# Zeros' products, alpha's operations and the first factors in the opening of a fused attention and snake-activation kernel

## Chip, cores and metric

One core of a Trainium2 chip runs the whole program. The metric is the time of one execution on the device in microseconds (us); a kernel is run three times or more, and the median counts. One more execution is taken by the profiler: its trace gives every instruction's start, length and waits, counted from the start of the span.

Engines: PE is TensorE (matrix products; PEld are its weight loads), ACT is ScalarE, DVE is VectorE, POOL is GpSimd, SP is SyncE, which only issues DMAs here. Each engine works through its own queue in order.

## What is computed

Cut to what matters, the reference is

```
scores = q @ k^T / 8 + bias[bucket(|i-j|)]        # 8 batches, 8 heads, 576 positions, 64 channels
attn   = softmax(scores);   x = attn @ v          # x: 4608 tokens x 512
h      = x @ w_in                                 # 512 -> 2048
g      = h + sin(alpha*h)^2 / (alpha + 1e-9)
out    = g @ w_out                                # 2048 -> 512
```

The bias depends on |i-j| and the head alone, and beyond distance 128 it is one constant. So the kernel uses exp(s + b) = exp(s) * exp(b), with exp(b) taken relative to the constant of the last bucket, which softmax cancels: only a band around the diagonal is multiplied by a factor, and the rest of the scores needs none.

## The kernel before

**Stages.** For each batch: scores (TensorE, into PSUM), exponentials (ACT, line 707), factors on the band (DVE, line 738; for the last 64 key positions, line 724, on DVE or POOL), AV products with a column of ones that gives the row sums, reciprocal and normalisation (DVE, lines 952 and 953), a turn of the normalised rows into xT. Then in blocks of 512 tokens: xT by w_in (plan_moe_in), sine (ACT, line 1068), square (line 1075 or 1077), g (DVE, line 1082), and g by w_out (plan_mo, 16 products of 512 columns for each 128 rows). Nearly all products are issued by one helper, so line 457 stands for scores, AV, both layers and zeros' products; tile names tell them apart.

**Order.** Nothing is ordered by hand. Each stage adds tasks to a Plan: an engine or several with a cost, dependencies, a priority, and `nb`, a time before which the planner doesn't place the task. `Plan.run` keeps a clock for each engine and places, at each step, the task that can start first; among those within 0.02 of it the lowest priority number goes first. It also hands out the PSUM banks: "sc" pairs (0,1), (2,3), (4,5) for scores, "h" single banks of these, "av" and "mo" banks 6 and 7. What it emits is an order in each engine's queue; on the chip only semaphores hold an instruction back. A due time thus moves an instruction in its queue and is no wait.

**The opening (batch 0).** Five things happen there.

- Lines 492 to 516: q and k of heads 0 and 1 are loaded, and cast on DVE and POOL. `warm(WARM0)` and `warm1(7, 192)` issue products of a tile of zeros (zz), 16 of 256 columns and WARM1 of 192, ahead of the first turn.
- plan_tr turns q and k of a pair of heads with TensorE (line 550 for the first pair, 556 for others) into an "mo" bank, and DVE copies it out (line 539). Due times are T_FIRST and T_PAIR.
- plan_table: a product of the bias table (32x32, 32x8), its exponential (line 595), a product that lays it out by distance, a copy to e_sb (line 605), a DMA to e_dram, and then the DMAs on SP that read it back as factor tables: m2r for heads 0-1, mhr (two DMAs), m2r for heads 2-3 and for heads 4-7, then v of heads 4 to 7.
- plan_att0: for each pair of heads five score units in the order of `runs`, A for 128 keys by 512 queries and two heads, C for the last 64 keys. Then AV and normalisation. `late` in plan_unit is the due time of a factor: T_MH for C units, T_M2[p] for A units of pair p.
- plan_alpha: a turn of alpha by TensorE (line 646) and three small DVE operations (lines 649 to 653) that give alphaT, which the sines read as scale, and inv_a, which line 1082 reads.

POOL issues the big loads: behind a one-element copy of m2r (line 633) w_in in four pieces, then q and k of batch 1 and w_out in four pieces (`loads2`), then v.

**Zeros' products.** Behind a task `Plan.run` tries one zeros' product for each entry of `m.pad`, with so many columns. `Plan.fill` takes the PSUM bank that has been free longest and gives up unless it has been free for WARM_LAG by the planner's clock:

```
        k = min((k for k in range(8) if fr[k] is not None), key=lambda k: fr[k], default=None)
        if k is None or fr[k] + WARM_LAG > now:
            return False
```

They take no time in the planner's clock and their results are never read.

Of the kernel before, what the change touches and what calls it, by code (L numbers as in the profile page):

```python
# [220 lines left out]
T_FIRST = (4.75, 5.95)  # L221
T_PAIR = ((7.9, 8.5), (9.3, 10.2), (11.6, 12.3))
T_ACT = ()
T_M2 = (15.0, 15.6, 16.8, 17.4)
T_MH = 15.2
T_RST = 25.0
T_V0 = (5.8, 6.4, 8.9, 9.6)
T_P3 = 7.0
T_VA = (10.5, 11.0)
T_VB = (19.5, 19.5, 19.5, 19.5)  # L230
T_AL = (10.0, 560)
LATE = 100
GA = 0.1
GB = 0.2
# [9 lines left out]
T_W = (25.5, 30.5)  # L244
T_WO = (40.5, 43.0, 45.7, 48.3)
WARM0 = 16
WARM1 = 4
WARM_LAG = 0.45
WARM_GAP = 0.12
WARM_FROM = 7.3  # L250
# [19 lines left out]
def kernel(  # L270
# [93 lines left out]
    def new_u():  # L364
        return tp.tile([128, 2, 9, 512], F16, name="u", tag="u", bufs=NBUF["u"])
# [18 lines left out]
    def bank(b, n=1):  # L384
        k = b.banks[0]
        return pb[:, k, :] if n == 1 else pb[:, k : k + n, :]
# [72 lines left out]
    def warm(n, k=7):  # L459
        for _ in range(n):  # L460
            full(pb[:, k, 0:256], zz[:, 0:128], zz, True, True)

    def warm1(k, n):
        full(pb[:, k, 0:n], zz[:, 0:128], zz[:, 0:n], True, True)
# [45 lines left out]
    warm(WARM0)  # L510
    for _ in range(WARM1):
        warm1(7, 192)
# [19 lines left out]
    def k_of(e):  # L532
        return {"ACT": nc.scalar, "DVE": nc.vector, "POOL": nc.gpsimd}[e]

    def copy_on(e, o, i):
        if e == "ACT":
            nc.scalar.activation(out=o, in_=i, func=AF.Copy)  # L537
        else:
            k_of(e).tensor_copy(out=o, in_=i)  # L539

    def plan_tr(t, p, kq, pri, nb, deps=()):

        b, c = Buf("mo"), Cell()

        def mm(e):
            c.v = bank(b).bitcast(F16)
            for i in range(SI):
                x = i * SN
                if t == 0 and p == 0:
                    nc.tensor.transpose(  # L550
                        out=c.v[:, x : x + SN], in_=natb[:, kq, i], identity=id_sb[0:SN, 0:SN]
                    )
                    continue
                for z in range(2):
                    h = 2 * p - 2 + z if t == 0 else 2 * p + z
                    nc.tensor.transpose(  # L556
                        out=c.v[64 * z : 64 * z + 64, x : x + SN],
                        in_=(nat1 if t == 0 else nat2)[:, kq, h, D * i : D * i + D],
                        identity=id_sb[0:SN, 0:SN],
                    )  # L560

        def cp(e):
            pin = c.v[:, 0:S].rearrange("d (i p) -> d p i", i=SI)

            dst = (kTs, qTs)[kq][t][:, p, :]
            copy_on(e, dst.rearrange("d (p i) -> d p i", i=SI), pin)

        m = plan.add({"PE": 0.4 if t == 0 and p == 0 else 0.5}, mm, deps, pri, nb, new=[b])
        if t == 0:
            m.pad = (256,) if p else (192,) * (3, 5)[kq]  # L570
        eng = {"DVE": 0.75, "ACT": 0.6}
        if t == 0:
            eng = {"ACT": 0.65} if p in T_ACT and kq else {"DVE": 0.75}
        x = plan.add(eng, cp, [m], pri, use=[b])
        if kq:
            return [x], [x]

        def tail(e):
            for z in range(2):
                r = slice(64 * z, 64 * z + 64)  # L580
                k_of(e).tensor_copy(
                    out=kts[t][r, p, r], in_=kTs[t][r, p, 512:S]
                )

        return [x], [plan.add({"POOL": 0.4 if t == 0 else 0.5}, tail, [x], pri + 30)]
# [55 lines left out]
    def plan_alpha():  # L641
# [12 lines left out]

        m = plan.add({"PE": 0.1}, mm, [], T_AL[1], nb=T_AL[0], new=[b])
        return plan.add({"DVE": 0.65}, cp, [m], T_AL[1], use=[b])

    def plan_unit(t, p, kind, c, u, ub, done, gate, base):
# [51 lines left out]
        x = plan.add({"ACT": n / 1200.0 + 0.065}, ex, [mark] + gate, base + 20, use=[b, ub])  # L710
        late = 0.0 if t else T_MH if kind == "C" else T_M2[p]
        if kind == "X":
# [43 lines left out]
    def run_time(units):  # L756

        kind = units[0][1]
        if kind in "CX":
            d = 0.13 if kind == "X" else 0.435 if units[0][3] else 0.22  # L760
            return d, [d]
        ends = [0.1 + 0.2185 * (k + 1) for k in range(len(units))]
        return ends[-1] + 0.11, ends

    def plan_att0(g, gates, gate):

        u, ub, done = Cell(), Buf("u"), {}
        a, b = 2 * g, 2 * g + 1
        runs = ((a, "A", 0), (a, "A", 1), (a, "A", 2), (a, "C", 0), (a, "A", 3),
                (b, "A", 0), (b, "A", 1), (b, "C", 0), (b, "A", 2), (b, "A", 3))  # L770
        exps, head = [], []
        for i, unit in enumerate(runs):
            base = PB + 3200 * g + 300 * i
            x = plan_unit(0, *unit, u, ub, done, gate, base)
            p, kind, _ = unit
            deps = gates + tr[(0, p, 0)][1 if kind == "C" else 0] + tr[(0, p, 1)][0]

            def run(e, i=i, x=x):
                if i == 0:
                    if g == 0:  # L780
                        plan.in_qk, plan.used = True, 0
                        plan.quota = QUOTA
                    u.v = new_u()
                plan.share = (g * len(runs) + i + 1) / (2 * len(runs))
                if g == 1 and i == len(runs) - 1:
                    plan.in_qk = False
                x[2](e)

            d, ends = run_time([unit + (False,)])
            m = plan.add({"PE": d}, run, deps, base, after=head,  # L790
                         new=([ub] if i == 0 else []) + [x[0]], use=[] if i == 0 else [ub])
            m.pad = (256,)
            m.offs = ([0.0] if i == 0 else []) + [0.1]
            m.marks = [(x[1], ends[0])]
            head = [m]
            exps += [x[3]]
        for p in (a, b):
            for w in range(2):
                base = PB + 3200 * g + 600 * ((2, 4)[w] if p == a else 4) + 50 * w
                plan_av(0, [(p, 256 * w), (p, 256 * w + 128)], u, ub, done, base, False)  # L800
        return exps
# [346 lines left out]

    PB = 0
    tr = {(0, 0, kq): plan_tr(0, 0, kq, -1000, T_FIRST[kq]) for kq in range(2)}  # L1150
    vdone, lds, spans = [], [], {}
    plan_table()
# [3 lines left out]
    for t in range(T):  # L1156
# [5 lines left out]
        for p in range(NP - 1) if t == 0 else ():  # L1162
            for kq in range(2):
                tr[(0, p + 1, kq)] = plan_tr(0, p + 1, kq, (150, 650, 5)[p], T_PAIR[p][kq])
        if t == 0:
            for g in range(2):
                exps += plan_att0(g, pe_gate, gate)
        else:
            exps += plan_att(t, pe_gate, gate)
            if t == 1:  # L1170
                exps += plan_late(PB + LATE, gate)
        if t == 0:
            for p in range(NP):
                for kq in range(2):
                    tr[(1, p, kq)] = plan_tr(1, p, kq, 10085 + 20 * p, T_TR1[kq])
            plan.add({"POOL": 5.0}, lambda e: stage_kq(2), [], 10090,
                     after=lds + [tr[(1, p, 0)][1][0] for p in range(NP)])
# [14 lines left out]
        for b in [t] if t < T - 1 else [t, t + 1]:  # L1192
            m, s_ = plan_moe_in(b, tbl)
# [36 lines left out]
```

## Time and profile before

| | |
|---|---|
| median of 3 runs | 373.41 us (372.92 to 374.12) |
| the profiled execution | 372.68 us, of which its span is 370.8 |
| PE busy | 363.3 us, 98% of the span |
| ACT busy | 316.9 us, 85% |
| DVE busy | 257.3 us, 69% |
| POOL busy | 91.5 us, 25% |
| granted TensorE clock by the page | 1.00 in all 40 slices (9 tenths or more) |

A busy PE counts products with modelled ends, so two products whose streams follow each other overlap in the table by some tenths of a us; steps from start to start say more. From 30 to 45 us PE is busy without a gap; in the opening the stretch from 14.4 to 17.8 is the thinnest, with 2.39 of 3.40 us. A line of the timeline reads: start, length, engine, line, operation, out<-in, shape, count, and in brackets the idle time before it with what ended it. A line of the chain of waits reads: start, length, what the end of the program was waiting for at that time. "issue" there is a time in which the profile shows no releaser.

### The profile page before, as it was taken

To read this page: it belongs to the slowest core of one execution; us is meant where nothing else is said; L and a number is where in the kernel's file an instruction comes from. 1 tells how busy PE (TensorE), PEld (TensorE's weight loads), DVE (VectorE), ACT (ScalarE), POOL (GpSimd) and SP (SyncE) were. 2 spreads that over 40 slices of the span, in tenths; PEclk is the share of its full clock that TensorE was granted. 3 is DMA by queue.
4 is the path that set the end of the run, shared out by engine and by line. 5 is a ranking of instruction groups with operands and counts; after the bars stand their busy time and mean duration, and the time that the engine had idled before them with its cause. 6 is when DMAs were issued, how large, how long until landed. Compare 5 with 4: busy or idle time off the path is not lost.

```text
span 370.8 us, 8950 instructions
## 1 busy us (share of the span) xinstructions
PE 363.3 (98%) x3588; PEld 196.9 (53%) x3588; DVE 257.3 (69%) x557; ACT 316.9 (85%) x433; POOL 91.5 (25%) x133
## 2 busy tenths in 40 slices
PE   8889999999999999999999999999999999999996
PEld 5464445644554455774554456445666455444443
DVE  4897957678677967696759866886769675979000
ACT  3998999899997999899979998899979997999111
POOL 7496350063000900072004600290005000000000
PEclk9999999999999999999999999999999999999999
DMA  9999999789625992399619992799259121000212
GB/s 165 211 166 203 200 174 121 149 68 134 111 58 114 93 189 67 83 147 139 112 49 147 135 144 58 134 114 165 76 111 92 65 68 39 7 30 2 82 61 86
DMA packets 149114, 40.49 MB, mean 109 GB/s; under 512 B 137080, under 2 KB 143568, under 8 KB 149072
## 3 DMA queue, kind: packets, MB, share of 16 engines
q0 software_dynamic: 96032, 17.67, 59.0%
q1 hardware_dynamic: 52864, 22.16, 24.4%
q8 instruction: 28, 0.46, 0.5%
q10 hardware_dynamic: 176, 0.09, 0.1%
q14 instruction: 14, 0.11, 0.1%
HBM read 37.73 MB, written 16.56 MB: 146 GB/s over the span
## 4 chain that ended last, share of the span: by engine, by line
PE 93%; ACT 4%; DVE 2%; issue 0%; ACTq 0%
PE pb L457 92%; ACT u L707 4%; PE pb L556 1%; DVE u L738 1%; PE pb L1024 1%; DVE xn L953 0%; DVE qT L539 0%; PE pb L550 0%; DVE xT L539 0%; DVE rd L952 0%; ACT outs L537 0%; ACT xT L537 0%; DVE zz L508 0%; PE pb L934 0%; ACTq L537 0%
## 5 line engine op out<-in xcount | busy, mean ns | idle before, releaser
L707 ACT ACTIVATE u<-pb 128x1024 f16<-128x1024 f32 (+1 forms) x146 | 137.3, 1022 | 7.9 <-PE pb L457 6.4
L457 PE MATMUL pb<-w_out,g 128*128 128x512 f16 (+2 forms) x592 | 139.2, 374 | 0.0
L457 PE MATMUL pb<-xT,w_in 128*128 128x512 f16 (+4 forms) x704 | 127.4, 340 | 0.0
L1082 DVE SCALAR_TENSOR_TENSOR g<-sq,inv_a,pb 128x512 f16<-128x512 f16 x144 | 101.3, 744 | 7.5 <-ACT sq L1075 3.6
L1068 ACT ACTIVATE s<-pb,alphaT 128x512 f16<-128x512 f32 x144 | 92.9, 690 | 11.8 <-PE pb L457 11.1
L457 PEld LDWEIGHTS <-w_in 128*128 128x128 f16 x704 | 64.7, 98 | 57.3
L457 PEld LDWEIGHTS <-g 128*128 128x128 f16 x592 | 53.9, 98 | 60.6 <-issue 6.2
L738 DVE TENSOR_TENSOR u<-u,m2r 128x512 f16<-128x512 f16 (+1 forms) x128 | 62.1, 491 | 33.7 <-ACT u L707 32.0
L457 PEld LDWEIGHTS <-u 128*128 128x128 f16 x1152 | 43.3, 97 | 9.6 <-issue 4.6
L402 POOL COPY kt<-kT 64x256 f16<-64x256 f16 x12 | 5.0, 414 | 171.0 <-DMA kT<-staged_k 148.9
L1075 ACT ACTIVATE sq<-s 128x512 f16<-128x512 f16 x72 | 44.7, 634 | 1.3 <-DVE g L1082 0.3
L457 PE MATMUL pb<-v,u 128*128 128x65 f16 x1024 | 43.7, 193 | 0.0
L457 PE MATMUL pb<-qT,kT 64*128 64x64 f16 (+1 forms) x512 | 41.7, 285 | 1.8 <-ACT u L707 1.2
L1077 DVE TENSOR_TENSOR sq<-s 128x512 f16<-128x512 f16 x72 | 29.7, 421 | 12.8 <-ACT s L1068 11.7
L953 DVE TENSOR_TENSOR xn<-pb,rd 128x256 f16<-128x256 f32 (+2 forms) x59 | 28.5, 483 | 2.0
L457 PEld LDWEIGHTS <-kT 64*128 64x128 f16 x512 | 16.2, 94 | 23.6 <-issue 16.9
L457 PE MATMUL pb<-vh,u 128*128 128x130 f16 x128 | 28.2, 221 | 0.0
L407 POOL DMA_DIRECT2D v<-in_v_dram x28 | 24.8, 893 | 5.1 <-DMA nat<-in_k_dram 2.4
L537 ACT ACTIVATE outs<-pb 128x512 f32<-128x512 f32 (+2 forms) x12 | 6.8, 569 | 19.9 <-PE pb L457 19.9
L952 DVE RECIPROCAL rd<-pb 128x4 f32<-128x4 f32 (+2 forms) x59 | 11.0, 186 | 13.3 <-PE pb L457 13.2
L539 DVE COPY outs<-pb 128x512 f32<-128x512 f32 x25 | 17.2, 686 | 4.0 <-PE pb L457 4.0
L1146 ACT ACT_TABLE_LOAD x15 | 19.2, 1283 | 0.3
(75 smaller groups left out, 186.6 us busy)
## 6 DMA issues: line engine op xcount, KB each, us to landing
out_dram<-outs SPq DMA_DIRECT2D x35, 256.0 KB, 2.7
v<-in_v_dram POOLq DMA_DIRECT2D x28, 128.0 KB, 4.7
staged_k<-in_k_dram POOLq DMA_DIRECT2D x6, 576.0 KB, 9.1
staged_q<-in_q_dram POOLq DMA_DIRECT2D x6, 576.0 KB, 12.1
w_in<-in_moe_w_in_dram POOLq DMA_DIRECT2D x4, 512.0 KB, 8.8
w_out<-in_moe_w_out_dram POOLq DMA_DIRECT2D x4, 512.0 KB, 15.7
w_out<-in_v_dram SPq DMA_DIRECT2D x6, 128.0 KB, 5.7
xT<-xn SPq DMA_TRANSPOSE x47, 2.6
```

The lines of the kernel that those rows point to most:

```text
L407: nc.gpsimd.dma_start(out=vs[t % 2][:, c, :, 0:D], in_=vp[128 * c : 128 * c + 128],)
L457: nc.tensor.matmul(out=out, lhsT=lhsT, rhs=rhs, start=start, stop=stop)
L539: k_of(e).tensor_copy(out=o, in_=i)
L707: nc.scalar.activation(out=o, in_=x, func=AF.Exp, scale=0.125)
L738: nc.vector.tensor_tensor(out=io, in0=io, in1=m2[:, 2 * p : 2 * p + 2, x0 : x0 + hi - lo], op=ALU.mult)
L952: nc.vector.reciprocal(out=r, in_=x[:, :, :, D])
L953: nc.vector.tensor_tensor(out=xn[:, 0:n].rearrange("p c (z d) -> p c z d", z=2), in0=x[:, :, :, 0:D], in1=r.unsqueeze(3).to_broadcast([128 ...
L1068: nc.scalar.activation(out=s16.v, in_=h.v, func=AF.Sin, scale=alphaT[:, f : f + 1])
L1075: nc.scalar.activation(out=sq.v, in_=s16.v, func=AF.Square)
L1077: k_of(e).tensor_tensor(out=sq.v, in0=s16.v, in1=s16.v, op=ALU.mult)
L1082: nc.vector.scalar_tensor_tensor(out=gcell[b].v[:, f, :], in0=sq.v, scalar=inv_a[:, f : f + 1], in1=h.v, op0=ALU.mult, op1=ALU.add,)
L1146: nc.scalar.preload_act_table_set(name)
```

## The change

Seven constants or pads change, and no function is new.

```
-T_M2 = (15.0, 15.6, 16.8, 17.4)
-T_MH = 15.2
+T_M2 = (14.2, 15.2, 16.4, 17.0)
+T_MH = 14.8
...
-T_AL = (10.0, 560)
+T_AL = (27.4, 10005)
...
-WARM1 = 4
+WARM1 = 3
+PAD0 = 160
...
         if t == 0:
-            m.pad = (256,) if p else (192,) * (3, 5)[kq]
+            m.pad = () if p else (192,) * (1, 7)[kq]
...
-            m.pad = (256,)
+            m.pad = (PAD0,)
```

The factors of batch 0 are due 0.4 to 0.8 sooner. Alpha's turn and its three DVE operations are due at 27.4 in place of 10.0, with a priority number behind the first products of w_in. One zeros' product fewer stands ahead of the first turn, one in place of three is tried behind the key turn of the first pair and seven in place of five behind its query turn, none behind the six turns of the other pairs, and behind each of the 20 score units of batch 0 one has 160 columns in place of 256.

## The prediction

> **What bounds the kernel now.** I read the chain of waits first, then the timeline of the opening engine by engine, then the weight tiles' transfers. The chain (start, length, what):
>
> ```profile
> 10.62 10.79 ACT u L707 x13
> ...
> 24.46 0.97 DVE u L738 x2
> ...
> 29.19 7.99 PE pb L457 x37
> ...
> 45.54 3.55 PE pb L457 x48
> 49.09 0.00 issue
> 49.09 4.46 PE pb L457 x54
> ```
>
> It has three parts. Until 24 us the exponentials (ACT, L707) set the pace. From 24 to 29 us DVE finishes factors and normalisations. From 29 us on it is TensorE, nearly without a break, to the end. So the change can only move the moment at which TensorE becomes continuous; the work behind it stays the same. The second thing to see is the break at 49.09, which is a wait, as the weight loads and the w_out tile's transfers show:
>
> ```profile
> 48.06 0.75 PEld L457 LDWEIGHTS <-g 128*128 128x128 f16 x4
> 49.09 0.74 PEld L457 LDWEIGHTS <-g 128*128 128x128 f16 x4 [0.28 <-issue]
> ```
>
> ```profile
> L443 POOL DMA_DIRECT2D w_out<-in_moe_w_out_dram x4: 755/765/770, 28.2 to 30.4; - x4
> ...
> DMA to landing us min/median/max: 12.8/15.7/18.6
> ```
>
> The last quarter of w_out is issued at 30.40 and lands 18.6 later, at 49.05; its first use starts at 49.09. The product before it starts at 48.71 and takes a step of 0.216, so TensorE would have been there at 48.92: it waits 0.17 us for a DMA. Ten big pieces (w_in four, next q and k, w_out four) land one behind the other between 23.8 and 49.05, each 2.5 to 3.5 us after the last, although each was issued up to 18.6 us ahead: a train whose speed the transfers set. Its head is released here:
>
> ```profile
> 18.32 0.18 POOL L633 COPY tick<-m2r 1x1 f16<-1x1 f16 x1 [1.46 <-DMA m2r<-e_dram]
> 18.55 2.90 POOL L438 DMA_DIRECT2D w_in<-in_moe_w_in_dram x4
> ```
>
> POOL waits for the last factor table (m2r of heads 4 to 7, issued 12.62, landed 18.26), then issues w_in. So the train moves only with the factor tables, and these with the table chain at the very start. TensorE in the opening:
>
> ```profile
> 5.16 0.52 PE L550 MATMUL pb<-id_sb,natx 96*128 96x96 f16 x6
> 5.52 0.41 PE L457 MATMUL pb<-zz 128*128 128x192 f16 x3
> 5.86 0.22 PE L457 MATMUL pb<-tabN,phi_sb 32*32 32x8 f32 x2
> 6.02 0.34 PE L457 MATMUL pb<-zz 128*128 128x192 f16 x2
> 6.34 0.37 PE L457 MATMUL pb<-phi_sb,tabE 32*8 32x512 f16 x1
> 6.65 0.43 PE L550 MATMUL pb<-id_sb,natx 96*128 96x96 f16 x6
> ...
> 7.93 0.39 PE L457 MATMUL pb<-qT,kT 64*128 64x512 f16 x2 [0.43 <-DVE qT L539]
> 8.25 0.28 PE L457 MATMUL pb<-zz 128*128 128x256 f16 x1
> 8.46 0.45 PE L556 MATMUL pb<-id_sb,nat 96*64 96x96 f16 x12
> 8.84 0.28 PE L457 MATMUL pb<-zz 128*128 128x256 f16 x1
> 9.06 0.39 PE L457 MATMUL pb<-qT,kT 64*128 64x512 f16 x2
> ```
>
> **The change, part by part.**
>
> *Zeros' products ahead of the table (WARM1 4 to 3; three to one behind the first turn).* One leading product steps 0.160 (four from 4.52 to 5.16). The first turn's weights load at 5.00, so it can start 0.16 sooner, but then all its six steps run at about 0.08 where the last two now run at 0.043: 0.08 is left. Two products fewer behind it: 2 x 0.083 = 0.17. tabN and phi landed at 3.6 and 5.0, so the bias product (5.86) waits for nothing but this queue: 0.08 + 0.17 = 0.25, of which I take 0.22. The exponential of the table, its product (6.34), the query turn (6.65), e_sb and the write to e_dram (issued 7.37) follow one behind the other, all 0.22 sooner. The query turn also needs POOL's cast, which ends at 6.18; by that it could come 0.4 sooner, so the cast does not bind. The seven products asked for behind that turn need free banks; by the planner's bank rule two of them find none, so five remain as now.
>
> *Zeros' products between turns and scores.* One of 256 columns costs 0.215 of TensorE's order (8.84 to 9.06); the six behind turns go. Those behind score units shrink by 96 columns, 0.04 each. The exponentials start at 8.36, 9.49, 10.62, 11.64, 12.23, 13.15, where later ones, back to back, step 0.904 (16.34, 17.25, 18.15) and a half one 0.477: 0.23 + 0.23 + 0.12 + 0.12 = 0.70 us are lost to late scores. A turn and its score would come 0.25 sooner per round (1.13 to 0.88), enough for ACT's own step.
>
> *Alpha moved.* Its product holds one of the two turn banks and 0.23 of TensorE; its three DVE operations take 11.91 to 12.58, 0.67. Without it, by the planner's rules, pair 2's query turn comes ahead of the first pair's last score instead of two scores later, and that score comes 0.38 later: some 0.3 of the 0.70 is given back. Exponentials: 0.22 + 0.70 - 0.30 = 0.6 sooner. DVE ends its turn copies near 14.2 instead of 15.3. At the new place the DVE operations follow the last normalisation (ends 28.63), where DVE is idle until 30.81, and the first sine (30.09) waits for its own product: nothing to pay. If they came ahead of that normalisation, TensorE would pay up to 0.67, but then waits less at 49.09. Alpha's DMA stays.
>
> *First factors sooner.* T_M2 and T_MH are due times, not waits, so they change order only. The first table lands at 14.54 (issued 10.18, 4.4 later), the last mhr at 16.22. DVE starts the first factor (15.22) near 14.35, runs three, and the fourth, the half unit's, stands at DVE's head until mhr is there: 16.0 to 16.3 instead of 16.50. Behind it are pair 0's last factor and pair 1's. The first AV moves ahead of two score units; its factor is there by 15.8, so scores are not held. DVE's idle 0.63 before 18.71 closes. POOL's half unit of pair 2 (21.81) stays behind the four w_in issues and moves only with them, 0.2, which holds the third pair's AV.
>
> *Sum in the opening.* ACT 0.6, reduced by that AV to 0.4 to 0.6: I take 0.45 sooner at 29.67. The first half of w_in is complete at 27.26, against a first use of 28.27 - 0.45, so it does not bind. All of this holds up to 48.92.
>
> *Sum at the end.* TensorE comes to the last quarter of w_out at 48.92 - 0.45 = 48.47. The train moves by what the tables move: 0.22 if they land as much sooner as they are issued, nothing if the loads beside them (v, landing at 15.89, the four v32) hold them; I take 0.2, since landings follow issues in order. So the quarter lands at 48.85, TensorE starts it at 48.89 instead of 49.09, and its wait grows from 0.17 to 0.4. Behind it the chain is TensorE up to 64.6: **0.2 us gained**, the rest given back at this wait. The profiled execution's 372.68 (span 370.8) would become 372.5; the median is 0.73 above that execution, so on the median 373.41 - 0.2 = 373.2.
>
> **The rivals.**
>
> *The opening's gain stays (20%).* The last quarter lands earlier, or its use falls behind other work. For it: the wait is only 0.17 now. Against it: ten landings at an even step. The opening gives 0.45 to 1.0 (1.0 is where w_in's landing at 27.26 stops it): 372.4 to 373.0, take 372.75. Beyond 1.1 us it takes, in addition, a faster train: 7 of the 20%.
>
> *It does not do what it says (16%).* The bias product starts no sooner, or the tables land when they do now; then the landing at 49.05 stands whatever the opening gains: 373.4.
>
> *The clock rises later (8%).* The zeros' products step 0.213 for 256 columns until 4.5 us and 0.083 for 192 after 5.5; inside the first turn the step falls from 0.087 to 0.043. So the clock doubles at about 5.4, with products back to back since 1.13. With four zeros' products fewer around that turn it may rise some us later. Then one product, a table product and a turn at half speed cost 0.08 + 0.21 + 0.22: the table chain is 0.1 later than now (0.08 + 0.21 - 0.22), and w_out with it: 373.5. [...]
>
> *Slower: the clock falls in the thin stretch (6%).* TensorE has least to do from 14.4 to 17.8 (busy 2.39 of 3.40, 20 products), and zeros' products are part of it. A pair needs 4 x 0.213 + 0.22 for scores and 4 x 0.30 + 0.14 for AV and turns, 2.4 us, beside 4 x 0.904 + 0.477 = 4.1 of ACT. At half the clock 4.8, so TensorE becomes the bound and each pair costs 0.7. It decides from two pairs on: one is paid by the 0.45 and the 0.17 at 49.09. Three pairs: 2.1 - 0.45 - 0.17 = 1.5, so 374.9. Against it: the AV moving forward fills that stretch, and the granted clock is 1.00 in every window now.
>
> **How the numbers follow.** Forecast 50%: 372.95 to 373.4, predicted 373.2. Rivals 20, 16, 8 and 6%. The range 372.3 to 374.0 leaves out the 7% and the 6%, and allows the spread of the three runs (372.92 to 374.12) in the median. A measurement of this kernel tells 0.3%, 1.12 us, from no change. Faster than 372.29: 7%, and 2% for gains that I have not seen: 9%. Slower than 374.53: 6%, and 1% likewise: 7%. Within: 84%.
>
> **What would show it.** The bias product at 5.64, e_dram issued at 7.15, exponentials 0.90 apart from the first, the first factor near 14.35, the half unit's factor on DVE at the mhr landing, POOL's copy of the table at 18.1, unbroken products by 29.2. Above all: the first w_out product of the last quarter still at a landing, at 48.9, behind a longer gap. If that gap is gone or the landing has moved by over 0.4 us, the forecast's main step is wrong. If the step of the zeros' products stays at 0.16 behind the first turn, the clock rival is right.

## The result, and the profile after

The changed kernel takes 374.11 us in median (22 executions, 372.72 to 375.92), the kernel before 373.04 us in as many beside it (372.36 to 374.24). The ratio is 1.0031 with a 95% interval of 1.0016 to 1.0045: slower by about 1.1 us, where 0.2 us less was forecast. Of the 22, five lie at 375.86 to 375.92 and the other seventeen at 372.72 to 374.90, with a mean of 373.84. The profiled execution is one of the five (375.92, span 374.0), and three more executions of the same kernel, each with its trace (373.37, 374.27 and 373.43, e13 to e15 below), show what the others look like. Helper lines have moved by one: 457 is 458, 707 is 708, 738 is 739, 952 and 953 are 953 and 954.

The chain of waits of the changed kernel, in time, columns as before:

```profile
12.73 0.67 PE pb L458 x3
13.40 0.62 PE pb L557 x11
14.02 1.57 PE pb L458 x6
15.59 1.10 PE pb L557 x24
16.69 5.79 PE pb L458 x54
...
32.88 7.50 PE pb L458 x34
```

Before, the exponentials carried the chain from 10.62 and TensorE became continuous at 29.19. Here TensorE itself carries it until 22.5, and the continuous stretch begins at 32.88. TensorE in the opening says why:

```profile
5.00 0.69 PE L551 MATMUL pb<-id_sb,natx 96*128 96x96 f16 x6
5.49 0.36 PE L458 MATMUL pb<-zz 128*128 128x192 f16 x1
5.78 0.27 PE L458 MATMUL pb<-tabN,phi_sb 32*32 32x8 f32 x2
5.98 0.50 PE L458 MATMUL pb<-zz 128*128 128x192 f16 x2
6.41 0.58 PE L458 MATMUL pb<-phi_sb,tabE 32*8 32x512 f16 x1
6.93 0.66 PE L551 MATMUL pb<-id_sb,natx 96*128 96x96 f16 x6
7.39 1.00 PE L458 MATMUL pb<-zz 128*128 128x192 f16 x5
```

The table product lasts 0.58 (0.37 before) and the second turn 0.66 (0.43): the doubling at 5.4 has not come. The trace's record of the granted clock puts it at 20.67. The last quarter of w_out lands at 50.41 here, and no product waits for it.

In the third of these further executions (e15) the clock doubles at 4.92, and the same stretch reads as forecast, with the wait for w_out at the end:

```profile
5.42 0.20 PE L458 MATMUL pb<-tabN,phi_sb 32*32 32x8 f32 x2
...
5.88 0.38 PE L458 MATMUL pb<-phi_sb,tabE 32*8 32x512 f16 x1
6.23 0.43 PE L551 MATMUL pb<-id_sb,natx 96*128 96x96 f16 x6
...
49.78 1.24 PE L458 MATMUL pb<-w_out,g 128*128 128x512 f16 x5 [0.61 <-DMA w_out<-in_moe_w_out_dram]
```

The bias product is 0.44 sooner than before (5.86), and the last quarter of w_out is waited for longer (0.61 in place of 0.17). Yet this execution's TensorE ends at 368.15, the one before at 367.46. So two things are to be found: what the clock does, and what the change costs when the clock is up in time.

One table serves all that follows. The 20 exponentials of batch 0 are numbered by their start; the first column of intervals holds what zeros, turns and scores do, the second what factors, AV and w_in do. Each row is one execution, so a difference between two rows holds the difference between executions too: the rows of e6 add up to 1.13 us over before, its median lies 0.16 us over it.

| kernel (profiled execution) | clock doubles at | 1st to 13th | 13th to 20th | 9th w_in product |
|---|---|---|---|---|
| before | 5.37 | 10.70 | 5.74 | 30.10 |
| changed | 20.67 | 13.21 | 6.01 | 33.31 |
| changed, e13 / e14 / e15 | 6.81 / 6.62 / 4.92 | 10.22 / 10.22 / 10.51 | 6.53 / 8.05 / 6.72 | 30.25 / 31.68 / 30.07 |
| e1 old zeros | 4.00 | 11.58 | 6.66 | 31.06 |
| e2 new zeros alone | 6.24 | 10.00 | 6.77 (clock halved 16.48 to 19.89) | 30.30 |
| e3 old lead | 6.29 | 10.21 | 6.62 | 30.48 |
| e4 old pads behind turns and scores | 4.77 | 11.58 | 6.66 | 31.17 |
| e5 AV later | 4.28 | 11.58 | 6.36 | 30.57 |
| e6 alpha alone | 7.03 | 11.58 | 5.99 | 31.40 |
| e7 due times alone | 5.70 | 10.70 | 6.29 | 30.53 |
| e8 few zeros | 6.22 | 10.78 (halved 9.63 to 16.46) | 8.14 | 32.08 |
| e9 v by DMA | no record | 10.45 | 7.52 | 31.72 |
| e10 tick, new order | 4.63 | 10.22 | 7.94 | 31.03 |
| e11, e16 before and tick | 6.38, 4.96 | 10.71, 10.70 | 5.74, 5.75 | 30.54, 29.91 |
| e12 short lead | 4.45, halved 7.86 to 18.10 | 13.21 | 5.73 | 32.13 |
| e17 tick, fewer zeros | 6.02 | 10.00 | 6.55 (halved 16.26 to 19.67) | 30.38 |
| e18 tick, more zeros | 6.98 | 10.70 | 5.75 | 30.68 |

### The profile page after: what moved, and what is told of

It reads as the page before. It is cut to its first block, busy times and chain, and to the rows that moved or that the text cites. A ratio compares the mean times of both kernels' runs of the same rounds, so it can differ in the third digit from the quotient of the medians.

```text
span 374.0 us, 8933 instructions
## 1 busy us (share of the span) xinstructions
PE 368.3 (98%) x3582; PEld 198.8 (53%) x3582; DVE 257.2 (69%) x558; ACT 316.9 (85%) x432; POOL 92.2 (25%) x133
## 4 chain that ended last, share of the span: by engine, by line
PE 96%; ACT 2%; DVE 1%; issue 0%; ACTq 0%; DVEq 0%
PE pb L458 93%; PE pb L557 2%; ACT u L708 1%; PE pb L1025 1%; DVE u L739 0%; PE pb L551 0%; DVE qT L540 0%; ACT xT L538 0%; DVE xn L954 0%; DVE xT L540 0%; ACT outs L538 0%; DVE rd L953 0%; DVE zz L509 0%; PE pb L647 0%; PE pb L935 0%
## 5 line engine op out<-in xcount | busy, mean ns | idle before, releaser
L458 PE MATMUL pb<-v,u 128*128 128x65 f16 x1024 | 44.6, 194 | 0.2 <-DVE u L739 0.2
L458 PE MATMUL pb<-qT,kT 64*128 64x64 f16 (+1 forms) x512 | 43.7, 293 | 0.1
L1078 DVE TENSOR_TENSOR sq<-s 128x512 f16<-128x512 f16 x72 | 29.6, 421 | 12.5 <-ACT s L1069 11.3
```

The lines of the kernel that those rows point to most:

```text
L458: nc.tensor.matmul(out=out, lhsT=lhsT, rhs=rhs, start=start, stop=stop)
L1078: k_of(e).tensor_tensor(out=sq.v, in0=s16.v, in1=s16.v, op=ALU.mult)
```

## The experiments

Two theories stood at the start. **Clock** (theory A in the texts below): the zeros' products taken away are what doubled TensorE's clock, and in some executions the doubling is missed. **Order** (theory B): alpha's new place and the earlier factors give TensorE another order, in which a product stands ahead of scores and waits. The rival to both: the opening gains, and transfers take it back. The runs of e1 to e4, of e5 to e8, of e9 to e12, of e13 to e16 and of e17 and e18 shared one chip each.

### e1: the changed order with all zeros as before

```
-WARM1 = 3            +WARM1 = 4
-PAD0 = 160           +PAD0 = 256
-m.pad = () if p else (192,) * (1, 7)[kq]
+m.pad = (256,) if p else (192,) * (3, 5)[kq]
```

> The changed kernel with all zeros' products as before (WARM1 4, three and five behind the first pair's turns, 256 columns behind the other turns and the score units); alpha and the due times stay changed. Theory A (the clock: with fewer zeros' products TensorE's clock rises later, in some executions only at 20 us): the loss goes, the median is at or below the kernel before, 372.6 to 373.1, and no execution is above 374.3. Theory B (the new order of turns, AVs and factors costs the time): still 374.1, 1.07 us over before. Theory C (both): in between, about 373.5.

Measured: 373.73 us (12 executions, 373.0 to 375.0; before 373.15), ratio 1.0023 (1.0008 to 1.0037). The clock doubles at 4.00 and the loss stays. The time lies between what theories C (both) and B had. So the order costs without any change of zeros: 10.70 + 5.74 becomes 11.58 + 6.66.

### e2: the kernel before with the new zeros alone

```
-WARM1 = 4            +WARM1 = 3
-m.pad = (256,) if p else (192,) * (3, 5)[kq]
+m.pad = () if p else (192,) * (1, 7)[kq]
-m.pad = (256,)       +m.pad = (160,)       # behind score units
```

> The kernel before with the changed zeros' products alone; alpha and the due times as before. Theory A: slower than before by about 1 us (374.1), executions spread from 372.7 to 375.9, and a profile that falls in a late execution shows zeros' products stepping 0.16 or more for 192 columns behind the first turn. Theory B: 373.0, spread as before (372.4 to 374.2). Theory C: about 373.5.

Measured: 373.08 us (372.17 to 374.0), ratio 0.9997 (0.9985 to 1.0009). This is theory B's time. None of the 12 lies near 375.9, although the zeros are those of the changed kernel. The first interval is 10.00 against 10.70: the 0.70 us that the exponentials lost to late scores are won to the hundredth. In the profiled execution they are lost again behind the 13th. The busy times by stretch of this kernel (bounds; length, busy time and count of PE, PEld, DVE, ACT, POOL; granted clock; DMA share; GB/s):

```profile
13.06:16.48 3.42, 2.29 (x24) 1.00 (x23) 2.45 (x5) 3.42 (x5) 0.46 (x2) 1.00 1.09 226
16.48:19.89 3.41, 3.14 (x42) 2.67 (x41) 2.71 (x9) 3.06 (x4) 2.17 (x5) 0.50 0.85 181
```

The share of a stretch in which products held TensorE's stream is counted here, turns left out, by their columns: 256 columns are 0.213 us at half the clock, the step of the leading zeros, and half of that at the full clock, where 512 columns step 0.216. The first of these two stretches has a share of 0.32, and the next 3.41 us run at half the clock (0.50): the 13th to the 14th exponential takes 1.84 in place of 0.90. This is the prediction's last rival, in the place it named. What it costs in the time of the whole is not shown: eight executions of e2 have a mean granted clock of 0.995 and average 373.07, the four without such a fall average 373.17.

### e3 and e4: the two places of the zeros apart

```
e3: WARM1 3 -> 4;  (192,) * (1, 7)[kq] -> (192,) * (3, 5)[kq]
e4: PAD0 160 -> 256;  () if p -> (256,) if p
```

> The changed kernel with the zeros' products ahead of and behind the first pair's turns as before (WARM1 4, three and five), those between turns and scores as changed. If the clock hangs on the first run of zeros' products (up to 7 us), this has before's time, 372.6 to 373.1. If it hangs on what follows from 8 us on, it stays at 374.1 with executions up to 375.9. Theory B: 374.1 with a narrow spread.

> The changed kernel with the zeros' products between turns and score units as before (256 columns behind turns and scores), those ahead of and behind the first pair's turns as changed. If the clock hangs on the stretch from 8 us on, this has before's time, 372.6 to 373.1, with executions up to 374.3; if on the first run alone, 374.1 with executions up to 375.9. Theory B: 374.1 with a narrow spread.

Measured: e3 374.12 us (373.0 to 375.18), ratio 1.0021 (1.0007 to 1.0036); e4 374.09 us (373.44 to 375.4), ratio 1.0031 (1.0018 to 1.0045). Both lie where theory B put them (374.1): neither takes the loss away. Neither has the group near 375.9 (highest 375.18 and 375.4), which would fit if both places of the zeros weigh on the missed doubling, but 12 executions of each without one, against five of 22, do not show it. In e3, with the clock up at 6.29, TensorE's order shows the stop:

```profile
21.78 0.22 PE L458 MATMUL pb<-vh,u 128*128 128x130 f16 x1
21.95 0.28 PE L458 MATMUL pb<-v,u 128*128 128x65 f16 x4
23.02 0.28 PE L458 MATMUL pb<-v,u 128*128 128x65 f16 x4 [0.79 <-POOL v L423]
...
23.43 0.38 PE L458 MATMUL pb<-qT,kt 128*128 128x256 f16 x2
23.74 0.39 PE L458 MATMUL pb<-qT,kT 64*128 64x512 f16 x2
```

The third pair's AV now stands ahead of the last pair's scores. It needs v of head 5, which POOL casts, and POOL is busy with this (the profile of e3, POOL):

```profile
18.34 0.18 POOL L634 COPY tick<-m2r 1x1 f16<-1x1 f16 x1 [2.14 <-DMA m2r<-e_dram]
18.57 2.92 POOL L439 DMA_DIRECT2D w_in<-in_moe_w_in_dram  x4
21.46 0.44 POOL L423 CAST v<-w_out 128x256 f16<-128x256 f32 x1
21.82 0.46 POOL L725 TENSOR_TENSOR u<-u,mhr 128x128 f16<-128x128 f16 x1
22.20 1.65 POOL L423 CAST v<-w_out 128x256 f16<-128x256 f32 x3
```

Four issues of w_in take 2.92 us of POOL, released by the tick, and only then come the casts. From the 16th to the 18th exponential ACT takes 2.61 us in place of 2.07, and from the 19th to the 20th, whose score stands behind the AV and the turns in TensorE's queue, 1.24 in place of 0.91. That POOL's cast holds this AV and that this is the loss is theory D in the texts below.

### e5: that AV behind two of the scores

```
e1 with  -T_V = ((15.5, 19.0), (50.0, 50.0))
         +T_V = ((15.5, 22.3), (50.0, 50.0))
```

> The changed order with all zeros' products as before (as e1), and the AVs of pairs 2 and 3 due at 22.3 in place of 19.0, so that pair 2's AV stands behind the last pair's half unit and its third score instead of ahead of them. Theory D (POOL: pair 2's AV waits for POOL's cast of v of head 5, which stands behind the four w_in issues; from 21.8 to 23.0 TensorE stands there with two score units queued behind it, ACT starves): the last exponential ends 0.5 us or more sooner than in e1, the loss of 0.6 goes, median 372.6 to 373.1. Rival (the loss comes from DVE, whose fourth factor stands at the head of its queue until mhr lands): no change against e1, 373.7.

Measured: 374.04 us (373.2 to 374.92), ratio 1.0022 (1.001 to 1.0033), so no gain, and theory D's 372.6 to 373.1 is missed. The 16th to the 18th exponential takes 2.07 again, and TensorE waits for no cast of POOL: that of head 5 ends at 23.38, the AV starts at 24.23. But TensorE now stands ahead of one of the last pair's scores for DVE's copy of a turn (TensorE, then DVE):

```profile
23.91 0.39 PE L458 MATMUL pb<-qT,kT 64*128 64x512 f16 x2 [0.65 <-DVE xT L540]
```

```profile
21.82 1.83 DVE L739 TENSOR_TENSOR u<-u,m2r 128x768 f16<-128x768 f16 x2
23.57 0.28 DVE L540 COPY xT<-pb 128x256 f16<-128x256 f16 x1
```

The copy stands on DVE behind two factors. TensorE's last score starts at 25.34, behind the moved AV, and the last exponential follows its predecessor by 1.42. One wait went, another came, and the ratio is that of e1: by this run the cast alone is not the loss.

### e6 and e7: the two changes of order apart, in the kernel before

```
e6: T_AL (10.0, 560) -> (27.4, 10005)
e7: T_M2, T_MH as in the change
```

> The kernel before with alpha's operations moved alone. By the planner's rules pair 2's AV stays behind the last pair's half unit and third score, so theory D sees no block: 372.7 to 373.1, 0 to 0.4 under before. Rival (the turn of pair 2's queries ahead of the first pair's last score starves ACT, and that is the loss): 373.5 or more.

> The kernel before with the due times of the first factors alone (T_M2, T_MH). By the planner's rules pair 2's AV stays behind the scores named, so theory D: as before, 372.9 to 373.3. Rival (DVE waits for mhr at its head): 373.5 or more.

Measured: e6 373.43 us (372.88 to 374.1), ratio 1.0005 (0.9995 to 1.0015); e7 373.31 us (372.36 to 374.68), ratio 1.0007 (0.9991 to 1.0023). Neither alone can be told from no change; together (e1) they can. In neither trace does TensorE wait for POOL's cast ahead of the last scores, so that wait needs both. The time of e6 lies between theory D's 372.7 to 373.1 and the rival's 373.5, that of e7 at the upper end of theory D's range. By the table alpha's move costs 0.88 in the first interval where the old zeros follow each turn, and the due times 0.55 in the second.

### e8: still fewer zeros

```
-m.pad = () if p else (192,) * (1, 7)[kq]     +m.pad = ()
-m.pad = (PAD0,)                              +m.pad = ()
```

> The changed kernel without any zeros' products behind turns of batch 0 and behind its score units (19 leading ones and two behind the bias product stay). Clock theory: the rise of the clock is missed in more executions than in the changed kernel, where 5 of 22 took 375.9: median 374.5 to 376, and a profile that took 375.5 or more shows 192-column zeros' products or turns at half step until AV begins (17 us or later), one that took less shows the rise by 8 us. Rival (the 375.9 executions have another cause): spread and median as in the changed kernel or less, 373.5 to 374.1.

Measured: 374.09 us (372.39 to 375.1), ratio 1.002 (1.0006 to 1.0035). The median is no later than that of the changed kernel, and none of the 12 lies near 375.9 (highest 375.1): both are what the rival had (373.5 to 374.1), and more missed doublings, which the clock theory expected, are not seen. What the profiled execution shows is a fall: the clock doubles at 6.22, falls at 9.63 after a stretch with products for 0.25 of its time, and rises at 16.46. The mean granted clock of an execution counts such falls: a stretch of 3.41 us at half the clock takes 3.41 / 2 / 371, or 0.0046, from it; the profiled executions of e2 and e17 have 0.995 with one, that of e12 0.986 with three. (Time ahead of the first doubling has no record and does not count: the profiled 375.92 has 1.00.) 8 of the 12 executions of e8 lie at 0.995 or lower, 8 of e2, 7 of e17, 6 of e12, 3 of e3, 2 of e11 and 1 each of e4, e10, e16 and e18, but none of the 60 of e1, e5, e6, e7 and e9 and none of over 120 of the kernel before in these runs. In e8 those with a fall average 374.07 and those without 374.13.

### e9, e10 and e11: what POOL does ahead of the casts

```
e9:  e3, v of heads 4 and 5 loaded by POOL's casting DMA (due 12.2), no SP load and no POOL cast
e10: e3 with  -P_.tensor_copy(out=tick, in_=m2r[0:1, 4, 0:1])
              +P_.tensor_copy(out=tick, in_=m2r[0:1, 2, 0:1])
e11: the kernel before with the same line
```

> The changed kernel with the lead of before (four products ahead, the zeros behind the first key turn as before: as in e3_old_lead) and with v of heads 4 and 5 cast by the load itself, so that no POOL copy behind the four w_in issues stands between it and pair 2's AV. If it is POOL's cast that holds pair 2's AV (in e3_old_lead PE stood from 21.8 to 23.0 for it), the stop is gone, the last exponential starts near 24.7 in place of 25.58, the ninth w_in product near 29.6 in place of 30.48, and then the last quarter of w_out (landing near 49) takes part of it back: 372.8 to 373.3 in median. If the stop only stands for something else (the bank, the exponentials, the query tile), nothing changes: 374.1. One more half unit is issued by POOL (about 0.7), which could put the w_in issues later by as much: then 373.5 to 374.

> As e3_old_lead, but the tick that lets POOL issue the four w_in loads is copied from the first query tile of heads 2 and 3 in place of that of heads 4 to 7, so that the issues, POOL's casts behind them and the train of w_in and w_out come about 1.2 us sooner. If POOL's casts behind the issues hold pair 2's AV, the stop is mostly gone and w_out is there sooner too: 372.6 to 373.0. If what costs is the order itself (turns ahead of score units), 374.1. Third: the w_in loads now compete with those of the second half of the first batch, whose keys and values come later: above 374.1.

> The kernel before with the same earlier tick and nothing else. In before nothing on PE's path waits for POOL's casts, so only the wait for the last quarter of w_out (0.17 in the profile) can go: 373.0 to 373.2, within 0.3% of 373.04. If the earlier w_in loads slow the loads of batch 0, it is above 373.5, and then the same must be taken off from what e10_tick2 gains.

Measured: e9 373.82 us (373.25 to 374.51), ratio 1.0003 (0.9988 to 1.0017); e10 373.2 us (372.59 to 374.99), ratio 0.9995 (0.9978 to 1.0012); e11 372.82 us (372.04 to 375.94), ratio 0.9991 (0.9966 to 1.0015). e3, with the stop, had 1.0021. e9 and e10 lie above their expected ranges (372.8 to 373.3, 372.6 to 373.0), e11 lies below its own (373.0 to 373.2). In e9 the AV runs through:

```profile
23.53 0.22 PE L458 MATMUL pb<-vh,u 128*128 128x130 f16 x1
23.59 0.40 PE L458 MATMUL pb<-v,u 128*128 128x65 f16 x8
23.83 0.22 PE L458 MATMUL pb<-vh,u 128*128 128x130 f16 x1
23.88 0.40 PE L458 MATMUL pb<-v,u 128*128 128x65 f16 x8
24.12 0.38 PE L458 MATMUL pb<-qT,kt 128*128 128x256 f16 x2
```

There is no idle time before any of them, and the 16th to the 18th exponential takes 2.07 as before the change: the cast was what held this AV. The profiled executions of e9 and e10 are no sooner for it, though (9th w_in product at 31.72 and 31.03; 29.6 was expected of e9). Both have a second stop, behind the 13th exponential, which e14 explains. In the profiled execution of e10 the tick came only 0.29 sooner than in e3 (18.05 against 18.34, where 1.2 was expected), since the table it copies landed at 17.99.

### e12: a shorter lead

```
-WARM1 = 3                 +WARM1 = 0
-(192,) * (1, 7)[kq]       +(192,) * (0, 7)[kq]
```

> The changed kernel with its first lead cut further: no products ahead and no zeros behind the first key turn. [...] If the late rise of the changed kernel has nothing to do with the zeros at its start, it is 374.1 with 2 or 3 of 12 near 375.9.

Measured: 375.07 us (372.48 to 375.8), ratio 1.0037 (1.0015 to 1.0059). Ten of twelve executions lie at 374.64 to 375.8 and two at 372.48 and 372.5. The rival's 374.1, for a late rise that has nothing to do with the zeros at the start, is not where the median lies. Of the ten, four (375.42 to 375.8) have a mean clock of 1.00, as the profiled execution with the missed doubling has, and six have 0.986 to 0.995, a fall. The profiled execution is one of the six: its clock rises at 4.45, falls at 7.86 after a stretch with 0.31 of products, and rises for good at 18.10. So a missed doubling is not seen in a trace of e12; it rests on those four.

### e13 to e15: three more executions of the changed kernel

No edit: the changed kernel itself.

> The changed kernel once more, for one look. If the clock's rise sets its time, an execution whose clock is up before 8 us lies between 372.7 and 374.5 and its last exponential starts by 26; one whose clock rises after 17 us lies at 375.9. If the time and the rise do not go together, the clock theory falls.

> As the look before it: a second pair of rise and time. In an execution with an early rise the stop of PE for POOL's cast of v of head 5 (near 22 to 23 us) must be there, since the order is the same; without it the order's cost has another place.

> As the two before it: a third pair of rise and time of the changed kernel.

Measured: 373.37, 374.27 and 373.43 us, with the clock doubled at 6.81, 6.62 and 4.92. With the profiled 375.92 at 20.67 there are four pairs, and all lie where the clock theory has them, with one miss: the last exponential of e14 starts at 26.78, not by 26. POOL's cast holds the third pair's AV in all three (released at 22.75, 24.17 and 22.57). e14, 0.9 us longer than the other two, has a second stop. TensorE, then DVE, in that execution:

```profile
18.13 0.41 PE L458 MATMUL pb<-v,u 128*128 128x65 f16 x8
19.83 0.29 PE L1025 MATMUL pb<-id_sb,xn 128*128 128x128 f16 x2 [1.29 <-ACT u L708]
...
23.14 0.28 PE L458 MATMUL pb<-v,u 128*128 128x65 f16 x4
24.21 0.28 PE L458 MATMUL pb<-v,u 128*128 128x65 f16 x4 [0.79 <-POOL v L423]
```

```profile
18.32 0.89 DVE L739 TENSOR_TENSOR u<-u,m2r 128x512 f16<-128x512 f16 x2 [1.01 <-DMA m2r<-e_dram]
19.14 0.18 DVE L953 RECIPROCAL rd<-pb 128x4 f32<-128x4 f32 x1
19.34 0.42 DVE L954 TENSOR_TENSOR xn<-pb,rd 128x256 f16<-128x256 f32 x1
```

TensorE has done the first pair's AV and next in its queue is the turn of the normalised rows, ahead of scores. The normalisation ends at 19.77 because it stands on DVE behind the second pair's factors, and these wait for the second m2r table, which landed at 18.23. The view puts TensorE's idle time down to an exponential, the 13th, which by the trace ends at 19.84, at the same time within 0.01. That it is DVE's normalisation shows in e8, e9 and e10: there the 13th exponential has ended 0.1 to 0.27 earlier, the view names DVE's xn, and the turn starts 0.05 to 0.06 behind the end of xn, as it does here. ACT pays:

```profile
16.92 2.92 ACT L708 ACTIVATE u<-pb 128x1024 f16<-128x1024 f32 x3
20.96 2.43 ACT L708 ACTIVATE u<-pb 128x512 f16<-128x512 f32 x3 [1.12 <-PE pb L458]
```

The stop comes and goes with the landing of that table against the 13th exponential. In e14, e8, e9 and e10 it landed within 0.5 us before it (18.23, 18.63, 18.77, 17.99), and the 13th to the 14th takes 2.2 to 2.5. In e1, e3, e4, e5, e13 and e15 it landed 1.8 to 2.3 before it (16.59 to 17.60), and the step is 0.90 to 1.20. (In e8, e9 and e10 DVE's wait for the same load ends at that landing.) The late landings begin at the issue: in these four SP's issue of the mhr load just ahead of that table takes 1.15 to 1.60 us, in the kernel before and in e15 0.60. In e15 another wait of DVE shows, the one that the prediction named: the half unit's factor stands at its head until mhr has landed (16.19), and the 14th exponential is 0.30 late. So in this order TensorE's path carries waits for loads that the order before did not.

### e16 to e18: the earlier tick again, with fewer and with more zeros

```
e16: as e11
e17: e11 with  (256,) if p -> () if p,  and (256,) -> (160,) behind score units
e18: e11 with  (192,) * (3, 5)[kq] -> (192,) * (3, 8)[kq]
```

> The kernel before with the earlier tick again, since ten of its twelve executions averaged 372.69 and two lay near 375.9. If the tick is a gain, the ratio comes out at 0.998 to 0.9995 again, with its bulk between 372.0 and 373.1; if the first result was chance, 1.000. If the executions near 375.9 come from the clock, none to three of twelve lie there.

> The kernel before with the earlier tick and, of the change, only the cut of the zeros behind the later turns (none in place of 256) and the score units (160 in place of 256); order and lead are those of before. If the cut zeros alone give the exponentials their 0.7 us in the old order and the earlier tick makes room for it at the end of the opening, the bulk lies near 372.0 and the ratio at 0.997 to 0.9985. If the cut zeros let the clock fall or leave it low in some executions, the bulk is no lower than in e16_before_tick2 (372.08 to 373.29) and more lie above 374.

> The kernel before with the earlier tick and three more products of zeros behind the second key turn (8 in place of 5, some 0.25 us at half clock each row of 192). If the executions near 375 to 376 of the earlier tick (3 of 22) are those in which no stretch of 3.4 us ahead of 10 us was full enough, they are gone (0 or 1 of 12), and the median stays within 0.4 of 372.67, later by what the three products hold up. If they have another cause, 1 to 3 of 12 stay there.

Measured: e16 372.45 us (10 executions, 372.08 to 375.13), ratio 0.999 (0.9973 to 1.0008); e17 373.04 us (371.95 to 376.17), ratio 1.0009 (0.9987 to 1.003); e18 372.86 us (372.3 to 376.61), ratio 0.9997 (0.9978 to 1.0016). e11 and e16 are one kernel: 22 executions with a median of 372.67, against 373.42 for 49 of the kernel before on the same chips; 19 lie at 372.04 to 373.71, three at 375.1 to 375.9, and these three have a mean granted clock of 0.995 where the others have 0.998 or more. The last quarter of w_out lands at 48.08 and 48.18 in place of 49.05, and nothing waits for it. The median gains, the ratio's intervals take in 1, so no version is shown to beat the kernel before. e17 wins the same 0.70 as e2 in the first interval (10.00) and loses it in the profiled execution to the same fall of the clock. The seven executions with the lower mean clock average 374.08, two of them near 376, and the five others 372.77, which is no sooner than the 19 of e11 and e16 (372.63): that the fewer zeros would gain without the fall is not shown. For e18 one of twelve stayed at 376.6, which decides nothing about those three. The 0.25 us that the text gives a row of 192 columns is the step of three at the full clock (0.083 each); at half the clock one steps 0.16.

## Why the prediction was wrong, step by step

**Zeros' products between turns and scores: right, to its size.** 0.70 was forecast and 0.70 measured (10.70 to 10.00 in e2 and e17).

**Alpha: right in order, near in size.** 0.30 was to be given back; e3, e13 and e14 give back 0.22 (10.22 against 10.00), e15 0.51. Alpha's DVE operations stand where the text put them, between the last normalisation and an idle DVE (28.34 to 29.10 in e15, first square at 30.78). With the old zeros behind each turn the same move costs 0.88 (e1, e4, e5, e6), a dependence that the text did not see.

**Table chain: right when the clock is up.** In e15 the bias product is at 5.42 (forecast 5.64), e_dram is issued at 6.91 (7.15) and POOL's copy starts at 17.93 (18.1). In the executions with the later doubling the write is issued at 7.53 to 7.65, behind the 7.37 of before.

**First factors sooner: wrong, and the main step that failed.** "The first AV moves ahead of two score units; its factor is there by 15.8, so scores are not held." The scores were not held there (ACT keeps its step of 0.90 up to the 13th exponential); what follows the AV was not weighed: the normalisation on DVE behind the next pair's factors, and the turn on TensorE ahead of scores. So with a landing at 18.0 to 18.8 ACT is held for 1.3 to 1.6 us. In the same way "POOL's half unit of pair 2 ... holds the third pair's AV" named the queue behind w_in's issues and took 0.0 to 0.2 for it, weighing the half unit and not the casts of v around it: the stop is 0.79 of TensorE in e3 and e14 and 0.4 in e13 and e15, and from the 16th to the 18th exponential ACT loses 0.54 in e3 and 0.32 to 0.62 in e13 to e15, and 0.33 more at the 20th. With this stop, and 0.1 to 0.3 more at the 14th exponential, the second interval grows from 5.74 to 6.53 and 6.72 (e13, e15), with the late landing as well to 8.05 (e14). The opening was to be 0.45 sooner; the 9th w_in product comes at 30.25, 31.68 and 30.07 against 30.10, so 0.45 sooner became 0.03 sooner to 1.58 later.

**The end: right as a place, wrong in size.** In e13 and e15 TensorE waits at the last quarter of w_out (0.37 and 0.61; 0.4 was forecast). But the quarter lands at 49.68 and 49.74, not 48.85, although the tick came 0.2 to 0.4 sooner: in e15 the first three quarters land at about the times of before (40.62, 43.74, 46.25 against 40.97, 43.76, 46.28) and the last 3.49 behind its predecessor instead of 2.77. That landings follow issues held for the train's head and not for its end. What stretched the last interval stays open; it is not the new order of the AVs, since e7 and e18, with the old one, have it too (3.42 and 3.96) and wait 0.30 and 0.26 there. That the wait of e13 has the forecast's size is luck: TensorE came to it at 49.35, not 48.47, and the landing had moved as far.

**The clock rival: right in kind, wrong in size.** It was given 0.1 us, a rise "some us later". Five of 22 executions are 2.0 us longer than the mean of the others, which is 5/22 x 2.0 = 0.47 of the mean's loss. Only one of the five has its trace, and in it the clock stays down until 20.67; that the other four do the same rests on their times and, for three of them, on a mean clock of 1.00 as in the traced one. e2, with the same zeros in the old order, has no such execution among 12, so that the zeros alone bring it is not shown. The sentence on the zeros' step staying at 0.16 behind the first turn came true in the profiled execution (five products behind the second turn last 1.00, and 0.58 in e15). In e8 the 3.41 us from 9.63 to 13.04 were 0.83 full with turns and 0.36 without, and the clock stayed at half; 13.04 to 16.46 was 0.78 full with turns and 0.72 without, and at its end the clock doubled. So in that trace the share without turns tells the two stretches apart and the share with turns does not, and turns are left out of the counts here.

**The fall of the clock: the rival was there.** It came at 16.48 in e2 and at 16.26 in e17, in the stretch named; with the changed order the AV fills that stretch, as was argued against it, and none of the four profiled executions of the changed kernel shows a fall. Four of its 22 have a mean clock of 0.995, so it happens in some. The price that it was given does not show in all: in e2 and e8 the executions with a fall are no slower than the others, in e17 they are.

**Sum.** In median 1.07 us was lost. The old order with the new zeros loses nothing (0.9997); the new order with the old zeros loses 0.0023, or 0.9 us; the rest, about 0.2 in the median, is put down to the missed doublings (without the five executions the median is 373.82, or 0.29 less). That the order costs, and the zeros alone do not, is shown by e1 and e2. Which of its waits carries the loss stays open. That the casts behind w_in hold the third pair's AV is shown by e9, whose stop vanished with them, and its time (1.0003 against 1.0021) points the same way, with intervals that overlap; but in e5 the wait for the cast is gone too and the time is not better (1.0022), and in its trace DVE's copy of a turn holds a score instead.

## What to carry to other kernels

Before a product is moved ahead in TensorE's queue, follow each of its operands to the engine that makes it and to what stands ahead there: a cast behind DMA issues (0.79 us of TensorE in e3) and a normalisation behind a factor that waits for a load (1.29 in e14) became waits of TensorE, and so of the exponentials. Taking one such wait away can let the next one through at the same price, as in e5 (1.0022, against 1.0023 in e1). Products that only keep the clock up are to be judged by what else stands in their stretch, not by their number: in e2, e8, e12 and e17 the clock fell at the end of 3.41 us with 0.25 to 0.32 of products, turns left out, though these runs fix no share that is enough. What one execution shows of the clock is one course of several: in the four traces of the changed kernel it first doubles at 4.92, 6.62, 6.81 and 20.67. Where a profile gives the clock as full from the start, as that of the changed kernel does, compare the steps of equal products, which tell the truth: five of 192 columns last 1.00 there and 0.58 in e15.

## What the runs showed of the hardware

The moves of the granted clock lie 3.41 us or a whole multiple of it apart: 10.24 and 3.41 in e2 (6.24, 16.48, 19.89), 3.41 and 6.83 in e8 (6.22, 9.63, 16.46), 3.41 and 10.24 in e12 (4.45, 7.86, 18.10), 10.24 and 3.41 in e17 (6.02, 16.26, 19.67), and up to the fall at the end 365.23 in before (5.37 to 370.59, 107 times 3.413) and 354.99 in the changed kernel (20.67 to 375.66, 104 times). Against the kernel's start the first doubling came at another time in every execution with a record (4.00 to 7.03, or 20.67).

In the 3.41 us ahead of a doubling products without turns held TensorE's stream for 0.94 of the time in before (1.95 to 5.37), 0.82 in the changed kernel (17.26 to 20.67), 0.76 in e2 and 0.72 in e6, e8, e13, e14 and e18, but for 0.57 in e12 (14.69 to 18.10). No doubling came after 0.67 in the changed kernel (3.61 to 7.02), nor after three first stretches at 0.71 to 0.73 (e18, the changed kernel and e6, 0.15 to 3.62). If each product counts up to the start of the next, the stretch of e12 has 0.73, but then 3.61 to 7.02 of the changed kernel has 0.83. So neither count tells the stretches ahead of a doubling from the others, and what decides it is not shown.

The 3.41 us ahead of a fall had 0.32 (e2), 0.31 (e12), 0.28 (e17) and 0.25 (e8) of products, and TensorE was not idle in them: 2.29 of 3.42 us busy in e2 (13.06 to 16.48). No fall came after 0.33 to 0.36 (e3, e10, e14, e18, e13, before).

The clock column of the busy times counts only what has a record. It shows 0.50 for a fall, as in e2 above, but 1.00 for the stretch before the first rise, which has none; in the profiled execution of the changed kernel, ahead of 20.67:

```profile
10.43:13.85 3.42, 3.42 (x45) 2.05 (x43) 1.79 (x3) 2.59 (x3) 2.13 (x6) 1.00 1.10 167
```

The second factor table landed at 16.49 to 18.77 in kernels that issue it alike, behind issues on SP at 11.48 to 13.65: a spread of 2.3 us in a load that one profile shows at a single time. The issues themselves are spread by 2.2 us; from issue to landing it took 4.5 to 5.7 us. In 15 of the 20 traces one of SP's issues of the last three factor loads took 0.9 to 1.6 us where these take 0.47 to 0.60 in before, and it was not always the same one.
